# Moving the split input of two fused feed-forward layers by 640 bytes inside SBUF

## The chip, the cores and the metric

The kernel runs on one core of one Trainium2 chip. The metric is the device time of one execution in microseconds (us). An engine's name in the rows of the profile: PE is TensorE's matmul stream, PEld its weight loads, DVE is VectorE, ACT is ScalarE, POOL is GpSimd, SP is the sync engine, which issues the transfers here.

## What is computed

Attention over 32 heads of 576 positions and 64 dimensions, then two feed-forward layers on the 2304 resulting rows of 512 numbers. Cut to what matters here:

```python
def _moe_ref(x, w_in, w_out):          # layer 0;  x: 2304 x 512, w_in: 512 x 2048, w_out: 2048 x 512
    h = x @ w_in
    g = h * np.cos(h)
    return (g @ w_out)

def _moe2_ref(x, w_in, w_out, s, b):   # layer 1
    h = x @ w_in
    r = np.maximum(h, 0.0)
    g = s * (r * r) + b
    return (g @ w_out)
```

The weights arrive as 64-bit numbers, and the kernel turns them into 32-bit ones by bit operations on ACT, POOL and DVE.

## The kernel before

**Attention** takes the first 256 us or so: sixteen pairs of heads, each with scores (L370, L377), a masked exponential, transposes (L334, L433) and the product with the values (`av`, L485).

**The feed-forward layers** fill the rest. The 2304 rows are cut into blocks of 512 columns and one of 256 (`blocks`, third in order). Within a block the 2048 hidden units are worked off in 16 pieces `f` of 128. The multiplications run in a format that keeps fewer bits than fp32, so each operand is split into a high and a low part, and each product is made of three matmuls: high by high, high by low, low by high. A piece has two groups of matmuls on PE:

- `h` (L753, function `hidden`): for each of four slices `c` of 128 rows of the input, three matmuls that hold a slice of the weights `wh` or `wl` (128x128) and stream the split input `x` of that slice (128x512, high or low) past it. Twelve matmuls, all into one bank of PSUM. In the short block two pieces share a step, so 24 matmuls of 256 columns.
- `acc` (L857 in layer 0, L859 in layer 1, function `output`): the activated piece `gh`, `gl` times the output weights, for each of four slices `d` three matmuls. In layer 0 a slice of the weights is held and `g` streams; in layer 1 a slice of `g` is held and the weights stream. Also twelve matmuls of 512 columns for a full block; in the short block 24 of 256 columns per pair of pieces in layer 0 and 12 of 512 in layer 1.

Between the two groups ACT, DVE and POOL make `r`, `gh` and `gl` of `h` (L783 to L836). The order of the instructions on each engine is set ahead of time by a planner (class `Order`) with a list of lengths and ranks; it does not know addresses.

**Where the operands lie.** Each tile is a run of bytes at one offset in all 128 partitions of SBUF. The tiles of the weights `wh`, `wl` and of `r`, `gh`, `gl` take 2048 bytes each, in pools that are filled from the low end. In the built program every one of them (128 of the weights, 144 of each of `r`, `gh`, `gl`) starts at an offset that leaves 1376 when divided by 2048; the weights lie between byte 46432 and byte 195936. The split input has four tiles `x0` to `x3` of 4096 bytes, one for each slice `c`, the high part in the first 2048 bytes and the low part in the second. They are made by `open_x` in a pool of their own at the high end, once the queries and keys of the attention are done with; they start at bytes 212960, 217056, 221152 and 225248, all of which leave 2016.

Each block's input is split into these four tiles anew: ACT rounds `xT` to the high part (L279 for line 727), DVE subtracts (L240 for line 730). A tile is filled for the next block once the last `h` group of the block has read it.

Of the kernel before, what the change touches and what calls it, by code (L numbers as in the profile page):

```python
# [10 lines left out]
F32 = mybir.dt.float32  # L11
# [7 lines left out]
P = 128  # L19
# [13 lines left out]
class Order:  # L33
# [26 lines left out]
    def add(self, engine, length, rank, fn, after=(), take=(), give=(), tail=None, mode=None, port=False):  # L60
        op = dict(
            mode=mode, port=port,
            n=len(self.ops), engine=engine, length=length, rank=rank, fn=fn,
            after=[a for a in after if a is not None], take=tuple(take), give=tuple(give),
            tail=self.TAIL.get(engine, 0) if tail is None else tail, start=None, end=None,
        )
        self.ops.append(op)
        return op
# [70 lines left out]


EARLY = 15
EARLY_WAY = "act"
LATE_WAY = "act"
HIGH = "ACT"
# [37 lines left out]
def attention_moe_moe2_kernel(  # L182
# [63 lines left out]
    def open_w(half):  # L246
        f, part = half
        wpools[half] = ctx.enter_context(tc.tile_pool(name=f"w{f}_{part}", bufs=1, reuse_waits="tile"))

    for half in halves[:EARLY]:  # L250
        open_w(half)
# [290 lines left out]
    def open_x():  # L542
        araw.release()
        pool = ctx.enter_context(tc.tile_pool(name="xp", bufs=1, side="right", reuse_waits="tile"))
        for c in range(HP):
            t = pool.tile([P, 2 * NB], F32R, tag=f"x{c}", name=f"x{c}")
            xtile.append((t[:, 0:NB], t[:, NB : 2 * NB]))

    def open_h():

        pairs = [ps_s.tile([P, 2, 512], F32, tag="s", name=f"h{j}") for j in range(2)]
        banks.extend(t[:, h] for h in range(2) for t in pairs)
# [4 lines left out]
    def open_rest():  # L557
        actx.close()
        for half in halves[EARLY:]:
            open_w(half)  # L560

    ox = add(None, 0, 0, open_x, after=[last_of["scores"]])
    oh = add(None, 0, 0, open_h, take=[ticket("s"), ticket("s")])
    oacc = add(None, 0, 1, open_acc, after=[oh], take=[ticket("pt") for _ in range(4)])
# [10 lines left out]
    def decode(half, rank, opened):  # L575
# [82 lines left out]
        early = opened is None  # L658
        way = EARLY_WAY if early else LATE_WAY if layer == 0 else "dve"
        l = add("SP", 60, rank - 6000, load, take=[tr], tail=4000)  # L660
# [20 lines left out]
    for j, half in enumerate(halves):  # L681
        if j < EARLY:
            decode((0, *half), PLACE["first"][j], None)
# [299 lines left out]
```

## Time and profile before

| | us |
|---|---|
| median of 3 runs (1057.98 to 1058.70) | 1058.54 |
| the profiled execution, its own time | 1058.82 |
| span in that execution, first to last instruction | 1057.0 |
| PE busy | 1038.1 (98% of the span) |
| DVE, ACT, POOL busy | 612.1, 504.1, 496.3 |

The page gives the busy time of each engine, then the chain of work that ended last (followed back from the last instruction), then groups of like instructions by source line with the mean duration of one. Matmuls are pipelined: the duration shown for one runs from its own start to its modelled end and overlaps the next, so the pace of a stream of matmuls is read from the distance between starts in the timeline, or from the pieces of the chain, not from the mean duration.

### The profile page before, as it was taken

How to read it: one execution, taken by the hardware profiler on the slowest of the kernel's cores; microseconds unless marked ns; L12 is line 12 of the kernel's file. 1: busy time of each engine (PE TensorE's matmuls, PEld its weight loads, DVE VectorE, ACT ScalarE, POOL GpSimd, SP SyncE). 2: the span in 40 equal slices, each digit the busy share in tenths (PEclk: the TensorE clock that was granted, in tenths of full speed). 3: DMA queues.
4: the chain of work that ended last, by engine and by line, in shares of the span. 5: the costliest groups of instructions: out<-in, count | busy, mean ns of one | idle time of the engine just before them, and what ended most of it. 6: DMA issues, size and time to landing. Idle time of an engine off the chain costs nothing.

```text
span 1057.0 us, 17568 instructions
## 1 busy us (share of the span) xinstructions
PE 1038.1 (98%) x6736; PEld 805.0 (76%) x6736; DVE 612.1 (58%) x1175; ACT 504.1 (48%) x927; POOL 496.3 (47%) x541
## 2 busy tenths in 40 slices
PE   6999999999999999999999999999999999999998
PEld 3665666666787888998887787887888888888886
DVE  7999999997778435444346778667211222113111
ACT  6999999996554222222234445444312322223221
POOL 3666666656886333333336776565222222222221
PEclk9999999999999999999999999999999999999999
DMA  5443444422332000000001232321100100001001
GB/s 177 136 153 121 139 153 139 145 63 87 120 100 78 22 0 21 1 1 21 0 1 41 80 100 81 100 80 60 40 1 1 40 1 21 0 1 40 1 1 40
DMA packets 23509, 63.61 MB, mean 60 GB/s; under 512 B 4464, under 2 KB 4736, under 8 KB 23424
## 3 DMA queue, kind: packets, MB, share of 16 engines
q1 hardware_dynamic: 23280, 62.48, 18.8%
q8 instruction: 53, 0.87, 0.3%
q14 instruction: 32, 0.26, 0.1%
q10 hardware_dynamic: 144, 0.00, 0.0%
HBM read 57.67 MB, written 4.79 MB: 59 GB/s over the span
## 4 chain that ended last, share of the span: by engine, by line
PE 88%; DVE 5%; ACT 3%; POOL 2%; issue 1%; DMA 1%; DVEq 0%; POOLq 0%; ACTq 0%
PE h L753 34%; PE acc L859 19%; PE acc L857 15%; PE av L485 7%; PE s L370 7%; PE pt L334 4%; DVE x L240 1%; PE ptr L433 1%; DMA wr<-in_w_dram 1%; PE s L377 1%; POOL r L796 1%; ACT e L396 1%; DVE r L804 1%; DVE wt L649 1%; DVE p L402 1%
## 5 line engine op out<-in xcount | busy, mean ns | idle before, releaser
L753 PE MATMUL h<-x,wh 128*128 128x512 f32 (+1 forms) x1280 | 370.5, 373 | 5.8 <-DVE r L804 3.6
L240 POOL TENSOR_TENSOR gl<-r,gh 128x512 fp32r<-128x512 f32 x144 | 193.5, 1344 | 326.5 <-DVE gh L827 252.9
L753 PEld LDWEIGHTS h<-x,wh 128*128 128x128 f32 x1280 | 231.2, 188 | 57.5 <-DVE r L804 8.0
L753 PE MATMUL h<-x,wl 128*128 128x512 f32 (+1 forms) x640 | 238.5, 373 | 0.0
L783 DVE TENSOR_SCALAR r<-r,s_t,b_t 128x512 f32<-128x512 f32 x72 | 43.9, 610 | 204.5 <-ACT r L279 202.8
L279 ACT ACTIVATE r<-h 128x512 f32<-128x512 f32 x72 | 43.0, 597 | 235.3 <-PE h L753 218.2
L753 PEld LDWEIGHTS h<-x,wl 128*128 128x128 f32 x640 | 120.2, 188 | 22.5
L279 ACT ACTIVATE r<-r,hpi 128x512 f32<-128x512 f32 x72 | 51.9, 720 | 155.3 <-POOL r L796 155.1
L402 DVE SCALAR_TENSOR_TENSOR p<-p,thr,e 128x576 f32<-128x576 f32 x144 | 118.1, 842 | 1.2 <-ACT e L396 0.2
L857 PE MATMUL acc<-gl,wh 128*128 128x512 f32 (+1 forms) x320 | 118.1, 369 | 0.0
L857 PE MATMUL acc<-gh,wl 128*128 128x512 f32 (+1 forms) x320 | 118.0, 369 | 0.0
L857 PE MATMUL acc<-gh,wh 128*128 128x512 f32 (+1 forms) x320 | 117.9, 368 | 0.0
L396 ACT ACTIVATE e<-p,mn 128x576 f32<-128x576 f32 x144 | 111.8, 778 | 10.0 <-DVE p L385 6.4
L859 PE MATMUL acc<-wh,gl 128*128 128x512 f32 x288 | 112.5, 391 | 0.0
L859 PE MATMUL acc<-wl,gh 128*128 128x512 f32 x288 | 112.4, 390 | 0.0
L859 PE MATMUL acc<-wh,gh 128*128 128x512 f32 x288 | 112.3, 390 | 0.0
L240 POOL TENSOR_TENSOR wl<-wt,wh 128x512 fp32r<-128x512 f32 x64 | 96.0, 1503 | 20.7 <-ACT wh L623 20.1
L385 DVE TENSOR_SCALAR_CACHE_REDUCE p<-s 128x576 f32<-128x576 f32 x144 | 104.1, 745 | 2.4 <-PE s L370 2.4
L392 POOL TENSOR_TENSOR thr<-mn,ptau 128x1 f32<-128x1 f32 x144 | 64.0, 449 | 75.6 <-DVE p L385 73.6
L370 PE MATMUL s<-ks,q 64*128 64x288 f32 x512 | 91.9, 446 | 7.5 <-ACT ks L314 5.5
L796 POOL TENSOR_SCALAR r<-r 128x512 f32<-128x512 f32 x72 | 50.1, 696 | 101.4 <-DVE r L793 99.7
L783 DVE TENSOR_SCALAR r<-h 128x512 int32<-128x512 f32 x72 | 49.6, 689 | 74.6 <-PE h L753 63.5
(70 smaller groups left out, 1461.8 us busy)
## 6 DMA issues: line engine op xcount, KB each, us to landing
wr<-in_w_dram SPq DMA_DIRECT2D x64, 512.0 KB, 3.7
q<-in_qt_dram SPq DMA_DIRECT2D x15, 576.0 KB, 5.6
v<-in_va_dram SPq DMA_DIRECT2D x16, 320.0 KB, 3.9
k<-in_kt_dram SPq DMA_DIRECT2D x16, 288.0 KB, 4.1
out_dram<-ob SPq DMA_DIRECT2D x18, 256.0 KB, 2.1
rb<-rd SPq DMA_DIRECT2D x16, 144.0 KB, 2.9
rb<-rd SPq DMA_DIRECT2D x16, 128.0 KB, 3.2
q<-in_qt_dram SPq DMA_DIRECT2D x1, 448.0 KB
```

The source lines that it names most:

```text
L240: (eng or nc.gpsimd).tensor_tensor(out=o, in0=a, in1=b.bitcast(F32), op=ALU.subtract)
L279: nc.scalar.activation(o, x, fn, **kw)
L370: nc.tensor.matmul(st[:, h, :H2], T["q"][g, c : c + 128], T["ks"][g, hd * H2 : (hd + 1) * H2], start=True, stop=True,)
L385: nc.vector.tensor_scalar(out=T["p", i], in0=T["s", i][:, :, :H2], scalar1=1.0, scalar2=None, op0=ALU.mult, op1=ALU.min, accum_out=T["mn", i],
L392: nc.gpsimd.tensor_tensor(out=T["thr", i], in0=T["mn", i], in1=ptau, op=ALU.add)
L396: nc.scalar.activation(T["e", i], T["p", i], AF.Exp, bias=T["mn", i], scale=-1.0)
L402: nc.vector.scalar_tensor_tensor(out=p, in0=p, scalar=T["thr", i], in1=T["e", i], op0=ALU.is_le, op1=ALU.mult, accum_out=T["sm"][:, i : i ...
L485: nc.tensor.matmul(T["av", h][g, :H2], T["v"][:, hd, k, :], T["PT"][:, 4 if k == 4 else k + 5 * hd, h * H2 : (h + 1) * H2], start=(k == 0) ...
L753: nc.tensor.matmul(B["h"][:, e * n : (e + 1) * n], wt[:, c * P : (c + 1) * P], x, start=(c == 0 and j == 0), stop=(c == HP - 1 and j == 2),)
L783: nc.vector.tensor_scalar(out=o, in0=x, scalar1=s1, scalar2=s2_, op0=ALU.mult, op1=ALU.add)
L857: nc.tensor.matmul(acc[d][:, :n], wt[:, d * P : (d + 1) * P], g, **st)
L859: nc.tensor.matmul(acc[d], g[:, d * P : (d + 1) * P], wt, **st)
```

## The change

An unused tile of 160 fp32 numbers (640 bytes) is allocated in the pool of the split input, after its four tiles. That pool sits at the high end of SBUF and grows downward, so the four tiles start 640 bytes lower.

```diff
 EARLY = 15
+
+XPAD = 160
 EARLY_WAY = "act"
...
         for c in range(HP):
             t = pool.tile([P, 2 * NB], F32R, tag=f"x{c}", name=f"x{c}")
             xtile.append((t[:, 0:NB], t[:, NB : 2 * NB]))
+        pool.tile([P, XPAD], F32, tag="xpad", name="xpad")
```

In the built program the tiles now start at bytes 212320, 216416, 220512 and 224608, all of which leave 1376 when divided by 2048. Nothing else of the program differs: no other tile moves, all 9658 instructions stand in the same order on every engine, and each waits for the same semaphores at the same values. The 640 bytes come out of a gap: the highest tile below them ends at byte 211456.

## Rows read from the trace of the kernel before

**Rows 1.** The page: busy time of the engines; the chain that ended last.

```profile
PE 1038.1 (98%) x6736; PEld 805.0 (76%) x6736; DVE 612.1 (58%) x1175; ACT 504.1 (48%) x927; POOL 496.3 (47%) x541
...
PE 88%; DVE 5%; ACT 3%; POOL 2%; issue 1%; DMA 1%; DVEq 0%; POOLq 0%; ACTq 0%
```

**Rows 2.** Busy us (and instructions) of each engine by stretch; then clock, DMA.

```profile
230.00:345.00 115.00, 110.72 (x584) 84.19 (x581) 91.14 (x122) 68.96 (x123) 84.99 (x80) 1.00 0.31 94
345.00:560.00 215.00, 215.00 (x1119) 183.73 (x1119) 96.60 (x140) 59.20 (x99) 77.61 (x82) 1.00 0.02 7
560.00:660.00 100.00, 98.29 (x422) 78.46 (x422) 77.89 (x103) 46.30 (x76) 69.59 (x65) 1.00 0.27 79
...
868.00:1042.00 174.00, 174.00 (x758) 141.77 (x757) 35.67 (x71) 42.21 (x69) 41.47 (x32) 1.00 0.03 10
```

**Rows 3.** The chain, in order of time, in block 5 of layer 1 (start, length, what).

```profile
929.06 2.79 PE h L753 x12
931.85 2.73 PE acc L859 x12
...
1039.59 2.79 PE h L753 x12
1042.38 10.91 PE acc L859 x48
```

**Rows 4.** Timeline of PE where the last `h` group meets the last four `acc` groups.

```profile
1041.75 0.40 PE L753 MATMUL h<-x,wh 128*128 128x512 f32 x1
1041.99 0.39 PE L753 MATMUL h<-x,wl 128*128 128x512 f32 x1
1042.22 0.39 PE L859 MATMUL acc<-wh,gh 128*128 128x512 f32 x1
...
1042.91 0.39 PE L859 MATMUL acc<-wh,gh 128*128 128x512 f32 x1
1043.14 0.39 PE L859 MATMUL acc<-wh,gl 128*128 128x512 f32 x1
...
1052.89 0.39 PE L859 MATMUL acc<-wl,gh 128*128 128x512 f32 x1
```

**Rows 5.** Groups of matmuls by line and form: busy, mean ns, idle before.

```profile
L753 PE MATMUL h<-x,wh 128*128 128x512 f32 x1024 | 323.9, 396 | 5.8 <-DVE r L804 3.6 <-DVE x L240 1.6
L753 PE MATMUL h<-x,wl 128*128 128x512 f32 x512 | 202.2, 395 | 0.0
...
L753 PE MATMUL h<-x,wh 128*128 128x256 f32 x256 | 46.6, 282 | 0.0
```

**Rows 6.** The chain in the short block of layer 0 (256 columns).

```profile
436.50 2.88 PE h L753 x24
439.37 2.88 PE acc L857 x24
442.25 2.85 PE h L753 x24
445.10 2.87 PE acc L857 x24
```

**Rows 7.** What PE waited for: 230 to 345 us, then 560 to 660 us.

```profile
PE h L753 <- DVE r L804: 2.5, 3, 0.9
PE h L753 <- DVE x L240: 1.3, 3, 0.6
...
PE h L753 <- DVE r L804: 1.1, 2, 0.9
PE h L753 <- DVE x L240: 0.3, 1, 0.3
```

**Rows 8.** Line 753 alone by stretch: busy us and instructions, PE then PEld.

```profile
230.00:345.00 115.00, 58.29 (x229) 42.06 (x230) 1.00 0.31 94
...
560.00:660.00 100.00, 53.27 (x214) 39.32 (x213) 1.00 0.27 79
```

**Rows 9.** Who writes the tiles `x`: ns min/median/max.

```profile
L279 ACT ACTIVATE x<-xT x40: 405/619/649, 235.8 to 954.5; 128x512 fp32r<-128x512 f32 x32, 128x256 fp32r<-128x256 f32 x8
L240 DVE TENSOR_TENSOR x<-xT,x x40: 408/687/1790, 236.9 to 955.2; 128x512 fp32r<-128x512 f32 x32, 128x256 fp32r<-128x256 f32 x8
```

**Rows 10.** Timeline of PE in the attention: `av` for pairs 0 and 1.

```profile
25.97 2.65 PE L485 MATMUL av<-PT,v 128*64 128x288 f32 x20
...
40.03 2.65 PE L485 MATMUL av<-PT,v 128*64 128x288 f32 x20
45.02 2.65 PE L485 MATMUL av<-PT,v 128*64 128x288 f32 x20
```

## The prediction

> **What bounds the kernel now.** I began with the page. PE is busy for 98% of the span, and 88% of the chain that ended last lies on it [rows 1]; no other engine comes near. So time can only be won by making PE's own stream shorter, or by taking out the few waits in it. The stretches say where those are [rows 2]: from 345 to 560 us and from 868 to 1042 us PE is busy without a break, at a granted clock of 1.00 (the 2.4 GHz level), while DVE works for less than half of the time and POOL, too. Between 230 and 345 us PE is idle for 4.3 us, between 560 and 660 us for 1.7 us. In both, the weights of a layer are being converted, and DVE has 91 of 115 us and 78 of 100 us to do.
>
> The change touches nothing but the address of what `h` streams. So I next asked whether the two kinds of matmul groups, which have the same shape and number, take the same time. They don't. In the chain a group `h` of twelve takes 2.79 us and a group `acc` of twelve 2.73 us [rows 3], 232.5 ns and 227.5 ns a matmul. Looked at closer the gap is larger. The last four `acc` groups follow each other with no `h` between them: from 1043.14 to 1052.89 us there are 43 distances in 9.75 us, 226.7 ns each, without a break in the pattern. The first three `acc` matmuls behind the `h` group take 0.69 us, 230 ns each, so what slows `h` still shows in the first three of `acc`. And inside `h` the distances alternate, 0.24 and 0.23 us at the end of the group [rows 4].
>
> **What the change removes, adds and moves.** It adds no instruction, removes none and moves none in the order; no wait is added and no transfer. The empty tile is never written or read and lies in a gap, so it costs nothing. What moves is the place of the four tiles `x`, from a remainder of 2016 to a remainder of 1376 modulo 2048. That is the remainder of both operands of every `acc` matmul: in layer 0 weights are held and `g` streams, in layer 1 the other way round, and both run at the pace of 226.7 ns once `h` is out of the way. `h` has the same shape, the same form of weight load and the same threefold pattern; of the two operands only `x` has another remainder. That is the case for the change.
>
> *The price of the present address.* From 929.06 to 1039.59 us the chain has 20 steps of one `h` and one `acc` group in 110.53 us, 5.527 us a step [rows 3]. At 226.7 ns throughout, 24 matmuls would take 5.442 us. The difference is 0.085 us a step. There are 1024 + 512 `h` matmuls of 512 columns [rows 5], which makes 128 steps, so **10.8 us** is what can be won at most.
>
> *The short blocks.* With 256 columns 24 `h` take 2.85 to 2.88 us and 24 `acc` 2.87 to 2.88 us [rows 6]: the same. I cost them at nothing. If `h` at the new address took 2.88 us each time, the 16 such groups would lose at most 16 x 0.03 = 0.5 us.
>
> *What is given back at waits.* Where PE waits for something that another chain of engines sets, an earlier PE only waits longer. From 230 to 345 us it waits 2.5 us for the product on DVE behind the cosine, and 1.3 us for `x` [rows 7]. There are 229 `h` matmuls in that stretch [rows 8], 19 steps, worth 19 x 0.085 = 1.6 us. Since the conversion of weights keeps DVE, ACT and POOL busy there, and it is not paced by PE, I take this to be lost altogether. From 560 to 660 us 214 matmuls, 18 steps, are worth 1.5 us, against 1.1 + 0.3 us of waits; there half of the work ahead of the waits is PE's own, so I take off half, 0.75 us. In the long stretches nothing waits: the next `h` group is ready long before PE comes to it, and what would be late first is DVE and ACT, which have over half of their time free [rows 2].
>
> *Writing the tiles.* Forty operations of ACT (619 ns) and forty of DVE (687 ns) fill `x` [rows 9]. The trace shows no such operation at the new address. As a bound, I let each become 10% faster or slower: 62 and 69 ns. PE waits for these writes at the changes of block, four tiles in a row, at nine blocks after the first: at most 9 x 4 x 0.13 = 4.7 us if all of it stood on the path, in either direction; but the waits for `x` come to 1.6 us in the whole trace [rows 5], so 10% of that, 0.2 us, is what I keep for the range.
>
> *The sum*: 10.8 - 1.6 - 0.75 = 8.4 us. The profiled execution took 1058.82 us, 0.28 us above the median, so 1050.4 us there and **1050.1 us** for a median.
>
> **The rivals.**
>
> *No change.* The slow pace of `h` may come from something else about `x`. The remainder isn't the only thing that sets these tiles apart: they lie above byte 212,000, while all weights lie below byte 195,936; and `h` gathers twelve products in one bank, where `acc` changes banks after three. The attention speaks for this rival: in `av` the streamed tile has a remainder of 1408 in pair 0 and 1664 in pair 1, the five parts of each lie 2304 bytes apart, and the values held lie 512 bytes apart from pair to pair, yet twenty matmuls take 2.65 us in every case [rows 10]. So an address alone doesn't slow a stream there, though that is another form, with 64 columns held. Against the bank: in `acc` two of three matmuls stay in the bank of the one before, and no distance in the steady pattern differs from the others. The time would be the median, 1058.5 us, within 1057.5 and 1059.5.
> The Trainium skill sides with this rival ("TensorE: Matmul & The Clock Gate", Step-by-step: what each phase is for): TensorE has two independent read ports of SBUF, one for the streamed operand and one for the weight load, and loading the next weights does not take read bandwidth from the running matmul. By that rule the two addresses could not disturb each other and the sum would be zero. The trace neither shows a conflict as such nor rules it out: it shows two paces for matmuls of one shape.
>
> *Slower.* If the disturbance comes where both reads run at the same remainder together, the change brings it about: the weight slices of `h` start at 1376 + 512c, and the streamed tile would begin level with one of them. Every `h` matmul would then take the long one of its two distances, 0.24 us [rows 4] in place of 232.5 ns: 1536 x 7.5 ns = 11.5 us, 1070 us. It decides as soon as the new remainder makes `h` slower than 232.5 ns. Against it stands that `acc` already has both operands at 1376 and is the fastest stream in the kernel.
>
> That the change doesn't do what it says is excluded: the built program has the tiles at the new remainder.
>
> **How the numbers follow.** The forecast gets 0.57: the pace differs between two streams that differ in little else, and the alternation looks like two reads that get in each other's way. No change gets 0.33, for the sake of `av` and of the other two differences; slower gets 0.10. Two runs of this kernel can be told apart from about 0.2%, 2.1 us. Every outcome of the forecast is beyond that, so the chances are 0.57 faster, 0.33 within 0.2%, 0.10 slower. The forecast's own range is from 1047.4 us (all of 10.8 us kept, and 0.3 us for writes and scatter) to 1053 us (half of 10.8 us). The range of all cases reaches from there to the no-change case: 1047.4 to 1059 us.
>
> **What would show it.** If the forecast is right, the chain shows `h` groups of twelve at 2.72 to 2.73 us in place of 2.79, the first three `acc` matmuls behind `h` at 227 ns, and a step at 5.44 us; the last `acc` run of 48 stays within 0.02 us of 10.91; the idle time between 230 and 345 us grows by up to 1.6 us. If `h` stays at 2.79 us, the remainder is not the cause and the second case holds. If the groups shrink, but the span doesn't, the waits of PE have taken the gain, and they would appear as longer waits for DVE in layer 0. It would be wrong altogether if `h` took 2.85 us or more.

## The result and the profile after

The changed kernel takes 1049.61 us (median of 4 runs, 1049.41 to 1050.41) against 1058.35 us (4 runs, 1057.98 to 1058.70): a ratio of 0.9919, with a 95% interval from 0.9902 to 0.9936. The forecast was 1050.1 us, in a range from 1047.4 to 1059. The profiled execution took 1049.41 us with a span of 1047.6 us; before it was 1058.82 and 1057.0. Line numbers of the changed kernel are two to three higher: `h` is L756, `acc` L860 and L862, DVE's product behind the cosine L807.

The page first, to be held against [rows 1]: the busy time of the engines, and the chain.

```profile
PE 1028.1 (98%) x6736; PEld 804.8 (77%) x6736; DVE 612.6 (58%) x1175; ACT 504.3 (48%) x927; POOL 497.9 (48%) x541
...
PE 84%; DVE 5%; POOL 4%; ACT 3%; issue 2%; DMA 1%; DVEq 0%; POOLq 0%; ACTq 0%; SPq 0%
```

PE has lost 10.0 us of busy time with the same number of instructions; no other engine's busy time moved by more than 1.6 us. The chain of block 5 in layer 1 answers to [rows 3]; columns are start, length, what.

```profile
926.92 2.72 PE h L756 x12
929.64 2.72 PE acc L862 x12
...
1030.28 2.72 PE h L756 x12
1033.00 10.89 PE acc L862 x48
```

Both groups now take 2.72 us. From 926.92 to 1030.28 us there are 19 steps in 103.36 us, 5.440 us a step in place of 5.527. In the timeline of PE, where the last `h` group meets the last `acc` groups [rows 4], the alternation and the three slow matmuls behind `h` are gone:

```profile
1031.93 0.39 PE L756 MATMUL h<-x,wl 128*128 128x512 f32 x1
1032.15 0.62 PE L756 MATMUL h<-x,wh 128*128 128x512 f32 x2
1032.61 0.39 PE L756 MATMUL h<-x,wl 128*128 128x512 f32 x1
1032.83 0.39 PE L862 MATMUL acc<-wh,gh 128*128 128x512 f32 x1
...
1033.51 0.39 PE L862 MATMUL acc<-wh,gh 128*128 128x512 f32 x1
```

Three `h` distances take 0.68 us and the three `acc` distances behind them 0.68 us; these three were 0.69.

Where the time went, stretch by stretch, is read from the same instruction in both traces. Three `h` matmuls behind a wait, in the changed kernel (timeline; the last column is the idle time before it and what ended it):

```profile
334.87 0.72 PE L756 MATMUL h<-x,wh 128*128 128x512 f32 x2 [0.89 <-DVE r L807]
567.15 0.72 PE L756 MATMUL h<-x,wh 128*128 128x512 f32 x2 [0.30 <-DVE r L807]
591.04 0.73 PE L756 MATMUL h<-x,wh 128*128 128x512 f32 x2 [0.85 <-DVE r L807]
```

and in the kernel before:

```profile
336.07 0.72 PE L753 MATMUL h<-x,wh 128*128 128x512 f32 x2 [0.87 <-DVE r L804]
570.85 0.72 PE L753 MATMUL h<-x,wh 128*128 128x512 f32 x2 [0.28 <-DVE r L804]
594.84 0.73 PE L753 MATMUL h<-x,wh 128*128 128x512 f32 x2 [0.85 <-DVE r L804]
```

They come 1.20, 3.70 and 3.80 us earlier, the first of the last 48 `acc` matmuls 9.39 us earlier (1042.22 [rows 4], 1032.83). Of the first 1.20 us, 0.4 us were there when `h` began (238.20 and 237.77 us), from the attention, which the change does not touch; over all runs here `h` begins anywhere between 237.8 and 238.6 us. So the stretch up to 336 us gave 0.8 us, from there to 571 us 2.5 us, and the rest 5.7 us.

The waits of PE, 228 to 342 us and then 556 to 656 us, answer to [rows 7]:

```profile
PE h L756 <- DVE r L807: 2.8, 4, 0.9
PE h L756 <- DVE x L242: 1.2, 3, 0.7
...
PE h L756 <- DVE r L807: 1.9, 4, 0.9
PE h L756 <- DVE x L242: 0.4, 1, 0.4
```

They have grown by 0.2 us in the first stretch and by 0.9 us in the second. Over the whole trace the idle time before `h` went from 5.8 [rows 5] to 6.7 us.

Both traces have the same 6736 matmuls in the same order, so the distances between starts can be compared one by one. From the first `h` on, distances of up to 300 ns in streams of 512 columns gave 10.2 us. Distances above 300 ns, that is the waits and the first matmul behind each, took back 1.1 us, and the short blocks 0.1 us. That makes the 9.0 us.

### The profile page after: what moved, and what is told of

The parts are those of the page before. It is cut to its first block, busy times and chain, and to the rows that moved or that the text cites. A ratio compares the mean times of both kernels' runs of the same rounds, so it can differ in the third digit from the quotient of the medians.

```text
span 1047.6 us, 17568 instructions
## 1 busy us (share of the span) xinstructions
PE 1028.1 (98%) x6736; PEld 804.8 (77%) x6736; DVE 612.6 (58%) x1175; ACT 504.3 (48%) x927; POOL 497.9 (48%) x541
## 4 chain that ended last, share of the span: by engine, by line
PE 84%; DVE 5%; POOL 4%; ACT 3%; issue 2%; DMA 1%; DVEq 0%; POOLq 0%; ACTq 0%; SPq 0%
PE h L756 32%; PE acc L862 19%; PE acc L860 14%; PE av L487 7%; PE s L372 7%; PE pt L336 4%; POOL wl L242 1%; DVE x L242 1%; POOL gl L242 1%; POOL r L799 1%; PE ptr L435 1%; PE s L379 1%; DVE wt L652 1%; DMA wr<-in_w_dram 1%; ACT e L398 1%
## 5 line engine op out<-in xcount | busy, mean ns | idle before, releaser
L756 PE MATMUL h<-x,wh 128*128 128x512 f32 (+1 forms) x1280 | 365.9, 370 | 6.7 <-DVE r L807 4.7
L756 PEld LDWEIGHTS h<-x,wh 128*128 128x128 f32 x1280 | 231.5, 189 | 54.7 <-DVE r L807 9.2
L756 PE MATMUL h<-x,wl 128*128 128x512 f32 (+1 forms) x640 | 235.6, 368 | 0.0
L756 PEld LDWEIGHTS h<-x,wl 128*128 128x128 f32 x640 | 120.7, 189 | 19.8
L860 PE MATMUL acc<-gl,wh 128*128 128x512 f32 (+1 forms) x320 | 117.7, 368 | 0.0
L860 PE MATMUL acc<-gh,wh 128*128 128x512 f32 (+1 forms) x320 | 117.7, 368 | 0.0
L860 PE MATMUL acc<-gh,wl 128*128 128x512 f32 (+1 forms) x320 | 117.7, 368 | 0.0
L862 PE MATMUL acc<-wh,gh 128*128 128x512 f32 x288 | 112.2, 389 | 0.0
L862 PE MATMUL acc<-wh,gl 128*128 128x512 f32 x288 | 112.1, 389 | 0.0
L862 PE MATMUL acc<-wl,gh 128*128 128x512 f32 x288 | 112.1, 389 | 0.0
L807 DVE TENSOR_TENSOR r<-h,r 128x512 f32<-128x512 f32 x72 | 49.6, 690 | 73.9 <-ACT r L281 69.1
```

The lines of the kernel that those rows point to most:

```text
L756: nc.tensor.matmul(B["h"][:, e * n : (e + 1) * n], wt[:, c * P : (c + 1) * P], x, start=(c == 0 and j == 0), stop=(c == HP - 1 and j == 2),)
L860: nc.tensor.matmul(acc[d][:, :n], wt[:, d * P : (d + 1) * P], g, **st)
L862: nc.tensor.matmul(acc[d], g[:, d * P : (d + 1) * P], wt, **st)
```

## The experiments

Each kernel is the changed one with the edit shown. Times are the run's own beside a run of the kernel before in the same job; e1 to e8, e11 and e12 are single runs, so their times say little below 0.2%, and the lengths of the groups in the trace carry the argument. "Distance" is the start of an input tile minus the remainder of the weight tiles, 1376; before, it was 640 bytes, with the change 0.

### e1, e2: other distances that are multiples of 256

```diff
-XPAD = 160
+XPAD = 32      # e1: distance 512
+XPAD = 96      # e2: distance 256
```

> The empty tile is 128 bytes instead of 640, so the input tiles leave 1888 modulo 2048: 512 bytes above the weights' 1376, the length of one held slice. Theory A (a relation modulo 2048 counts, the tiles have to lie level with the weight tiles): the input is as unlevel as before, an h group of twelve takes about 2.79 us, the time is about 1058. Theory B (a relation of the two operands modulo 512 or a divisor of it counts, since the four held slices lie 512 apart and none was special): 2.72 us a group and about 1049.5. Theory C (the streamed tile's own remainder counts, whatever the weights' is): open, between 2.72 and 2.79.

> The empty tile is 384 bytes, the input tiles leave 1632: 256 bytes above the weights. Before, they were 640 = 512 + 128 above them. If B holds with a period of 256 or 128 bytes, an h group takes 2.72 us and the whole 1049.5; if its period is 512, the groups stay above 2.72, perhaps at 2.79 (1058) or at some third value. A expects about 2.79.

Measured: 1050.15 us (e1) and 1049.62 us (e2), beside 1058.44 before. The chain in block 5 of layer 1, e1 and then e2:

```profile
903.18 2.72 PE acc L862 x12
905.90 2.72 PE h L756 x12
```

```profile
902.61 2.72 PE acc L862 x12
905.33 2.72 PE h L756 x12
```

An empty tile of 128 bytes does what the one of 640 does. Theory A falls: the input need not lie level with the weight tiles modulo 2048. B holds, with a period of 256 bytes or a part of it; since 640 is slow and leaves 128, a period, if there is one, is 256; e5 to e8 try what lies between. From here on two operands are called level when their starts differ by a multiple of 256 bytes, and off level otherwise.

### e3: all tiles at the remainder that was slow

```diff
+    cpool.tile([P, XPAD], F32, name="cpad")
     tau_t = cpool.tile([P, 1], F32, name="tau_t")
...
-        pool.tile([P, XPAD], F32, tag="xpad", name="xpad")
```

> No empty tile at the input, but 640 empty bytes at the low end of SBUF: weights, g, r and the input all leave 2016. A and B (the relation counts): both groups at 2.72 us as with the change, about 1049.5 us. C (the streamed tile's own remainder counts): h stays at 2.79, and acc, whose operands now leave 2016 too, rises to 2.79 as well: some 128 x 0.07 + 10.8 us more than with the change, about 1066. The rival that the tiles' other properties slowed h is out already, but would expect no change against before.

Measured: 1050.29 us. (The expectation's own terms for C come to 1069 us, not 1066; nothing hangs on it.) The input starts at the same bytes as before the change, 212960 and so on; only the tiles it meets have moved.

```profile
903.30 2.72 PE acc L862 x12
906.02 2.72 PE h L756 x12
```

Theory C falls, and with it every reason that lies in the input's own place, the high end of SBUF included. What counts is the relation of the held and the streamed operand.

### e4: the disturbance put into the other group

```diff
+    gpad = ctx.enter_context(tc.tile_pool(name="gpad", bufs=1))
+    gpad.tile([P, XPAD], F32, name="gpad")
     mg = ctx.enter_context(tc.tile_pool(name="mg", bufs=2))
...
         actx.close()
+        wpad = ctx.enter_context(tc.tile_pool(name="wpad", bufs=1, reuse_waits="tile"))
+        wpad.tile([P, 512 - XPAD], F32, name="wpad")
```

The second tile puts the late weight tiles back to 1376.

> The change stays, but gh and gl move to a remainder of 2016 while all weights and the input stay at 1376. So h is level and acc is 640 off: in layer 0 the streamed operand, in layer 1 the held one. A and B expect acc in layer 0 at 2.79 us a group instead of 2.72 and in layer 1 slower too, if it is the distance and not its sign that counts; h at 2.72 with a slow start behind each acc group; about 1058 to 1060 us if both layers slow, about 1054 if only layer 0 does. If only the input's place at the high end counted, the time stays at 1049.5.

Measured: 1059.89 us, 1.4 us above before. The chain in layer 0, where `g` streams, and in layer 1, where `g` is held and the weights stream:

```profile
294.89 2.73 PE h L760 x12
297.63 2.79 PE acc L864 x12
...
901.63 2.76 PE h L760 x12
904.39 2.80 PE acc L866 x12
```

`acc` has become the slow group in both layers. So the effect can be put where one likes, and moving either of the two operands brings it about. Layer 0 is the mirror image of before: the steady distances of `acc` are 237 and 229 ns in turn, as those of `h` were, and the first three `h` matmuls behind it are slow, 2.73 us for the group. With the held operand moved, in layer 1, the price is a little higher, and `h`, which is level, takes 2.76 us, with slow matmuls beyond the third.

Layer 1 shows one thing more. The last `h` matmul of a group has both its own operands level, but in the trace the load of the next weights, the moved `g`, starts with it, both at 903.99 us. The distance to the next start is 232 or 233 ns in all 59 groups that run without a wait. In layer 0, where the next weights are level with the running stream, it is 226 or 227 ns in 47 of 48. That fits a stream that is slowed by the load for the matmul behind it; how, no run shows.

### e5 to e8: small distances

```diff
-XPAD = 160
+XPAD = 152     # e5: distance 32
+XPAD = 144     # e6: distance 64
+XPAD = 176     # e7: distance -64
+XPAD = 136     # e8: distance 96
```

> The input tiles leave 1408, 32 bytes above the weights. Distances of 512, 256 and 0 gave 2.72 us an h group, 640 (128 modulo 256) gave 2.79. Theory D (two reads collide unless they are a multiple of 256 bytes apart): slower than 2.72, some 2.74 to 2.80, 1052 to 1060 us. Theory E (they collide only at or near half the period, 128): 2.72 us, 1049.5. Theory F (level operands are themselves a compromise, and the 13 ns a matmul above the slope between 256 and 512 columns is a collision too): some distance gives less than 226.7 ns a matmul, here or in the next three runs.

> The input tiles leave 1440, 64 bytes above the weights. D: slower than 2.72 us an h group, E: 2.72 or between it and 2.79, F: perhaps below 2.72. If the bank of a read were set by bits above 64 bytes only, 32 bytes would cost less than 64.

> The input tiles leave 1312, 64 bytes below the weights. If only the size of the distance counts, the same pace as with 64 bytes above; if the two reads chase each other through the banks, one direction is better than the other. D: slower than 2.72 us a group; E: 2.72 or a little above; F: perhaps below.

> The input tiles leave 1472, 96 bytes above the weights, nearest to the 128 modulo 256 of before. D and E: 2.75 to 2.80 us an h group, 1053 to 1060 us.

Measured: 1060.41, 1057.90, 1058.51 and 1063.83 us, beside 1059.01 before. The short blocks, which have their own rule (e9), are in these times too, so that e6 and e7 come out below before although a full step is no shorter. An `acc` and an `h` group of each, from the chain in block 5 of layer 1, in the order e5, e6, e7, e8:

```profile
904.97 2.76 PE acc L862 x12
907.72 2.80 PE h L756 x12
```

```profile
903.10 2.77 PE acc L862 x12
905.87 2.76 PE h L756 x12
```

```profile
903.56 2.74 PE acc L862 x12
906.30 2.80 PE h L756 x12
```

```profile
902.44 2.76 PE acc L862 x12
905.20 2.81 PE h L756 x12
```

| distance (bytes) | `h` + `acc`, us | run |
|---|---|---|
| 0, 256, 512 | 2.72 + 2.72 = 5.44 | change, e3; e2; e1 |
| 640 (128 modulo 256) | 2.79 + 2.73 = 5.53 (its two rows give 5.52) | before |
| 64 | 2.76 + 2.77 = 5.53 | e6 |
| -64 | 2.80 + 2.74 = 5.54 | e7 |
| 32 | 2.80 + 2.76 = 5.56 | e5 |
| 96 | 2.81 + 2.76 = 5.57 | e8 |

Theory D holds: every distance tried that isn't a multiple of 256 costs 0.09 to 0.13 us a step. Half the period is not the worst (E falls), and 32 bytes are enough. The two directions differ (64 and -64). For streams of 512 columns no distance beat level operands, so F falls there. It has something in it for the short blocks, which e9 takes up.

### e9: the short blocks off level, the full ones level

```diff
-        n = blocks[blk]
+        n = blocks[blk]; xo = 48 if n < NB else 0
...
-                act(xtile[c][0][:, :n], xT[:, c, a:b], AF.Copy)
+                act(xtile[c][0][:, xo : xo + n], xT[:, c, a:b], AF.Copy)
...
-                xh, xl = (t[:, :n] for t in xtile[c])
+                xh, xl = (t[:, xo : xo + n] for t in xtile[c])
```

The low part is moved in the same way.

> As the change, but in the short blocks (256 columns) the split input begins 192 bytes further inside its tiles, 64 below a multiple of 256 against the weights; full blocks stay level. In the run with all input 64 below, a step of the short blocks took 5.55 us in layer 0's last four and in layer 1 against 5.62 to 5.76 with the change. If the short stream has its own rule (a level stream of 256 columns runs at 120 ns, one off level at 117), the steps shrink by 0.07 to 0.15 us and about 1 to 1.5 us of the whole is won, 1048.3, if what follows a short group does not lose its pace; full h groups stay at 2.72 us. If the quick steps of that run were an effect of its slow full blocks, the short steps stay at 5.62 to 5.76 and the time at 1049.6 or above.

Measured: 1048.49 us (median of 4, 1047.81 to 1049.18) against 1058.25 before (median of 7), a ratio of 0.991 (0.9893 to 0.9926). The chain in the short block of layer 0 of the changed kernel, to be held against [rows 6], and of layer 1:

```profile
439.88 2.88 PE h L756 x24
442.76 2.88 PE acc L860 x24
...
816.68 2.87 PE h L756 x24
819.55 2.75 PE acc L862 x12
```

and of e9:

```profile
439.53 2.74 PE h L756 x24
442.27 2.86 PE acc L860 x24
...
826.73 2.83 PE h L756 x24
829.56 2.72 PE acc L862 x12
```

A step is shorter by 0.16 us in the first and by 0.07 us in the second, and the median fell by 1.1 us, as expected. At 64 bytes below level, streams of 256 columns take 114 to 118 ns a matmul against 120 level. That isn't simply the opposite rule: in the other runs they take 117 to 118 ns at distances of 32 and 64, but 119 to 120 at 640 (before [rows 6]) and 120 at 96. The short block of layer 0 in e8:

```profile
448.89 2.88 PE h L756 x24
451.77 2.88 PE acc L860 x24
```

So for the short stream some distances are quicker than level and others are not; why, no run here settles. e9 is the fastest version tried, but the interval of its ratio overlaps with that of the change, so that it beats it rests on the trace.

### e10: the planner told the new pace

```diff
-                    "PE", 3 * (18 + n / 2.4), rank, hidden_part, mode="all",
+                    "PE", 3 * (15 + n / 2.4), rank, hidden_part, mode="all",
```

> As the change, but the planner is told the new pace of h: 15 ns in place of 18 above the slope for a matmul, 226.7 + 1.6 in all. Groups keep 2.72 us. Some waits of PE between 230 and 345 and between 560 and 660 us move; the change's trace has 8.9 us more in distances above 262 ns before and in h than a steady pace, and the new order may take away or add one or two of them: 1046 to 1053 us. If the waits are set by the other engines' work alone, as the prediction held, the order of PE changes nothing: 1049.6 within 1 us.

Measured: 1050.56 us (median of 4, 1050.40 to 1050.86), 0.9 us above the change. The group of `h` matmuls in e10 (busy, mean ns, idle before):

```profile
L756 PE MATMUL h<-x,wh 128*128 128x512 f32 x1024 | 318.3, 391 | 8.2 <-DVE r L807 5.7 <-DVE x L242 2.5
```

The idle time before `h` is 8.2 us against 6.7 with the change. The order planned with the truer length has more waits, not fewer. But the planner orders every engine, and the new number moved instructions of POOL, ACT and DVE as well: POOL's order differs from 260 us on, PE's own only from 321 us. Between 228 and 318 us, where PE still works in the order of the change, what `h` waits for DVE's product has already grown from 1.9 us in three waits to 2.6 us in four:

```profile
PE h L756 <- DVE r L807: 2.6, 4, 0.9
```

So the waits depend on the order planned for the engines together. Whether PE's own order has a part in it, this run does not show.

### e11: both groups off level

```diff
+    gpad = ctx.enter_context(tc.tile_pool(name="gpad", bufs=1))
+    gpad.tile([P, XPAD], F32, name="gpad")
     mg = ctx.enter_context(tc.tile_pool(name="mg", bufs=2))
...
-        pool.tile([P, XPAD], F32, tag="xpad", name="xpad")
```

with the second tile of e4 as well.

> No empty tile at the input, and gh and gl are moved to the remainder of 2016: both groups now have one operand 640 bytes off, h as before, acc as in the run with g moved. If each group pays for its own distance, a step takes twice 2.79 us, 5.59, against 5.53 before and 5.44 with the change: 128 x 0.06 = 8 us above before, less what waits absorb, 1063 to 1067 us. If a stream off level only loses when it has to find its pace again behind a level one, both groups off would cost no more than one: 1058 to 1060.

Measured: 1062.86 us, beside 1058.25 before. The chain in block 5 of layer 1:

```profile
901.46 2.78 PE acc L865 x12
904.24 2.78 PE h L759 x12
```

Three steps take 16.70 us (895.89 to 912.59 us), 5.57 us each, 0.04 above before and 0.13 above the change. Both groups pay, by about 0.06 us each; 128 steps of 0.04 us are 5 us above before, and 4.6 were measured. The time is just below the range expected, since a step is 0.02 us shorter than the 5.59 us that it was to take. It may be that with nothing level left the passage from one group to the other costs nothing extra; the run does not separate that from a lower price of each group.

### e12: only the low part of the input off level

```diff
-XPAD = 160
+XPAD = 32
...
-            t = pool.tile([P, 2 * NB], F32R, tag=f"x{c}", name=f"x{c}")
-            xtile.append((t[:, 0:NB], t[:, NB : 2 * NB]))
+            t = pool.tile([P, 2 * NB + 64], F32R, tag=f"x{c}", name=f"x{c}")
+            xtile.append((t[:, 0:NB], t[:, NB + 32 : 2 * NB + 32]))
```

> The high part of the input is level with the weights (as with the change), the low part lies 128 bytes off modulo 256 (as both did before). In each slice the low part streams in one matmul of three. If every matmul pays only for its own distance, an h group loses a third of what it lost before: 2.72 + 0.07 / 3 = 2.74 to 2.75 us, and the time is about 1049.6 + 128 x 0.028 = 1053. If one stream out of step throws the following ones out as well, until they have found the pace again (some ten matmuls after a wait), the group stays near 2.79 and the time near 1058.

Measured: 1051.71 us, beside 1058.81 before. The chain and the timeline of PE in block 5 of layer 1:

```profile
904.10 2.72 PE acc L862 x12
906.82 2.75 PE h L756 x12
```

```profile
906.65 0.62 PE L756 MATMUL h<-x,wh 128*128 128x512 f32 x2
907.12 0.39 PE L756 MATMUL h<-x,wl 128*128 128x512 f32 x1
907.34 0.62 PE L756 MATMUL h<-x,wh 128*128 128x512 f32 x2
907.80 0.39 PE L756 MATMUL h<-x,wl 128*128 128x512 f32 x1
```

`h` takes 2.75 us, and the three matmuls of a slice take 0.69 us (907.12 to 907.80 is 0.68, 906.65 to 907.34 is 0.69) in place of 0.68. Start by start the distances of the steady groups are 227, 234 and 226 ns in turn, and the long one is that of the low part: one of three pays, and it alone. A matmul loses 7 ns for its own distance and does not throw the next ones out. The whole was 1.3 us quicker than 1053; the short blocks, whose low part is off level too, are quicker (their 24 `h` take 2.82 us), which the expectation had left out.

## Why the prediction was right

- *PE's own stream bounds the kernel, and the address of `x` sets the pace of `h`.* Right. That no other tile and no place in the order moves made the comparison clean; e3 and e4 show that it is the relation to the weights and not the place of the tile.
- *The price of the present address, 10.8 us at most.* The pace fell to what the term took for it, 5.440 us a step against 5.442, also in the first three `acc` matmuls. From 336 to 571 us, where PE hardly waits, the trace of before has 34 full steps, worth 34 x 0.085 = 2.9 us, and 2.5 us were won.
- *What is given back at waits, 1.6 + 0.75 us.* Near in size, but partly by luck: the reason given held in one stretch of two. Behind the attention 9.4 - 0.4 = 9.0 us were won of the 10.8, so 1.8 us were given back, against 2.35. Only 0.9 us of that is longer idle time before `h`: the stretch up to 336 us, which was to give nothing, gave 0.8 us, and its waits grew by 0.2 us instead of 1.6. What the step had missed there is in the rows: the product that `h` waits for at 336.07 us came 1.20 us earlier itself, 0.8 us more than `h` had begun earlier, so that chain, too, seems to be paced in part by PE. In the second stretch the waits grew by 0.9 us where 0.75 was taken off. The rest of the 1.8 us had no term in the sum. Most of it goes with matmuls of 512 columns that don't run at 226.7 ns although their operands are level, those behind a wait above all (last section) and the groups next to short ones, 2.75 us instead of 2.72 (e9). That the page now has 4% of the chain on POOL instead of 2% fits the half of the argument that held: in places the conversion of weights, and not PE, may be what ends last.
- *The short blocks and the writes, nothing.* Right in size. The two writes take 618 and 686 ns, against 619 and 687 [rows 9]. The short `h` groups rose from 2.85 or 2.88 to 2.87 or 2.88 us, as bounded. That they could be made quicker, e9 had to show.
- *The sum.* 8.4 us forecast, 8.7 us measured between the medians; 9.4 us between the profiled executions, of which 0.4 us come from the attention and have nothing to do with the change. So 9.0 us were won where 8.4 were forecast.
- *No change, 0.33.* It rested on `av` [rows 10]. Those rows are true, but the differences that it named, 256 bytes between the remainders, 2304 between the parts and 512 between the values held, are all multiples of 256, so they could not have shown the effect. The two halves of a part, 288 columns each, do start 1152 bytes apart, which leaves 128. So in the built program half of the twenty matmuls are level and half are not, and behind the first pair all of them start in pairs, 242 or 243 ns from pair to pair. That form, with 64 columns held, is indeed not slowed, but nothing about the form of `h` follows from it. Its other supports, the place at the high end and the one bank of twelve products, fall with e3, where both are as before and `h` takes 2.72 us.
- The Trainium skill ("TensorE: Matmul & The Clock Gate", Step-by-step: what each phase is for) has two independent read ports and no loss from the next weight load. Here the measurement decides: the same matmul takes 227 or 233 ns according to the distance of its two operands modulo 256 bytes. The last `h` matmul of a group in layer 1 of e4 fits a collision of the next weight load with the running stream: its own operands are level, and it is slowed. What inside the reads collides isn't shown by any run.
- *Slower, 0.10.* It supposed that level operands collide. They are the best of the distances tried for 512 columns. An address that is worse than the one of before does exist: at a distance of 96 bytes the kernel was slower (1063.8 us).

## What to carry to other kernels

Where PE is the bound and two streams of matmuls of one shape run at different paces, compare the start addresses of the held and the streamed operand: here, with 128x128 held and 512 columns streamed, every pair that differs by a multiple of 256 bytes ran at 226.7 ns where the groups around it did so too, every other pair tried at 230 to 235 on average over a group. Other forms need a trial of their own: the streams of 256 columns were quicker at some distances off level, and `av` showed no difference. Such a thing is read from the distance between starts; the mean duration of a matmul, 396 ns for `h` in [rows 5], holds the overlap with the next and gives no pace. Here an unused tile of 128 bytes cured it (e1). Before costing what a faster engine gives back at its waits, ask how much of the awaited work that engine paces itself.

## What was not expected of the hardware

- For streams of 512 columns past 128x128 the period is 256 bytes, not the 2048 of a tile, and 32 bytes off level cost as much as 128: 2.80 and 2.79 us a group of twelve.
- Streams of 256 columns have another rule: 120 ns level, 114 to 118 ns at 64 below, 117 to 118 at 32 and 64 above, and 120 again at 96.
- The price is paid matmul by matmul (e12: 7 ns for the one of three), yet at the passage between two groups it shows up to three matmuls late (before) and longer at small distances: with 64 bytes the level group behind an off-level one takes 2.77 us instead of 2.72.
- A matmul whose own operands are level takes some 5 ns longer to the next start where the weights loaded meanwhile are off level with its stream (e4, the last `h` of each group: 232 ns in layer 1, 227 in layer 0).
- Behind a wait even level operands need some five (591.04 us) to ten (567.15 us) matmuls to reach 226.7 ns: in the changed kernel the twelve behind the wait at 567.15 us run to the first `acc` at 570.02 us, 2.87 us, where twelve in step take 2.72.

The last row of this, the first `acc` behind that wait:

```profile
570.02 0.39 PE L860 MATMUL acc<-gh,wh 128*128 128x512 f32 x1
```
